# Dot products of the seventh attention tile behind the sixth tile, fixed attention steps in the first two blocks, and first halo columns on VectorE

## The chip, the cores and the metric

The kernel runs on one core of one Trainium2 chip. The metric is the device time of one execution in microseconds (us). Five engines work in parallel, each through its own queue in order: TensorE (PE: matrix products into PSUM), VectorE (DVE), ScalarE (ACT), GpSimd (POOL) and SyncE (SP, which issues the DMA transfers here). They wait for one another through semaphores.

## What is computed

Three stages follow each other: a linear attention with a decaying state, a gated feed-forward mixer with a convolution over three time steps, and a normalised feed-forward mixer with a residual.

```python
# B, H, S, D = 4, 8, 768, 48; d_model = 384, d_ff = 1024
for t in range(S):                                  # attention
    cur = einsum('bhd,bhe->bhde', u * k[t], v[t])
    y[:, :, t] = einsum('bhd,bhde->bhe', r[t], state + cur)
    state = w * state + einsum('bhd,bhe->bhde', k[t], v[t])
h = maximum(x @ w_in, 0)                            # mixer 1, x is y
conv = sum over taps 0..2 of conv_w[tap] * h shifted by tap - 1 (zeros at the ends of a sequence)
x = (h * sigmoid(conv)) @ w_out
xn = (x - mean) / sqrt(var + 1e-6) * g_ln           # mixer 2
out = x + maximum(xn @ w_ch1, 0) @ w_ch2
```

## The kernel before, in words

**Tiles and blocks.** Time is cut into 24 attention tiles of 128 steps (index n from 0, six to a sequence; the sixth tile is n = 5, the seventh n = 6). Mixer 1 works in eight blocks of 384 steps, that is of three tiles (index j), mixer 2 in six blocks of 512. Every product of the mixers is made three times, of high and low parts (`xh` and `xl`, `wih` and `wil`, `gh` and `gl`), for precision.

**Mixer 1.** For each of eight slices f, nine matmuls fill `psm` (here called an up product); ScalarE takes the positive part (`h`) and the middle tap (`c`), VectorE adds the two other taps (L474, `c<-h,tables,c`), ScalarE takes the sigmoid, VectorE multiplies by `h` (L455), ScalarE and VectorE split the result into `gh` (L460) and `gl` (L461), and nine matmuls add it into `acc` (a down product), which runs two to three slices behind the up products. An up product reads the block's three tiles and one column more on either side, the halo. `halos` (L279) copies that column between the blocks' tiles or sets it to zero, all of it on GpSimd (lines 284 to 290).

**Attention.** The function `attention` is a generator; each `yield` ends a step. A tile goes through stages: its r and k are multiplied by decay tables (L347, `rk<-rk,tables`) and its diagonal is made; then the dot products (`dps`, eight matmuls) with their mask; then the product `yps` that gives `xh` and `xl`. `state_update` (matmuls `pst`) carries the state to the next tile. Tiles below LIGHT = 6 take a form that leaves more to GpSimd and ScalarE; from tile 6 on ScalarE writes eight diagonal blocks (L358) and VectorE the masked copies (L363). For a tile n from 6 on, `decayed_k` (L249, `kks<-kt,tables`) multiplies its k by tables, twice as wide as before.

**The order around the change.** The first tiles run alone; then `after1`, called sixteen times in a mixer-1 block, advances `attention` by one step whenever a running sum `pace` passes 5: six steps in block 0 (calls 3, 6, 8, 11, 14 and 16) and seven in block 1. The weights are decoded alongside from packed words (`wdec`, `wil`, `wol`; VectorE, with a part on GpSimd and ScalarE). Matmuls stand on TensorE in program order; instructions called through `vo`, `ao`, `so` and `go` keep program order too, while a scheduler that estimates times places the others (`v_`, `a_`, `g_`, `nc.sync`) among them.

Of the kernel before, what the change touches and what calls it, by code (L numbers as in the profile page):

```python
# [35 lines left out]
LAG = 3  # L36
EARLY = 4
LIGHT = 6
GC = 16
GE = 4  # L40
SMALL = 3 * NP + KT
# [7 lines left out]
def body(ctx, tc, r, k, v, w, u, w_in, conv_w, w_out, g_ln, w_ch1, w_ch2, rkT, krv, small, out):  # L49
    nc = tc.nc  # L50
# [14 lines left out]
    g_ = nc.gpsimd  # L65
# [12 lines left out]
    vo = InOrder(nc.vector)  # L78
# [129 lines left out]
    def wdo(count=1, last=None):  # L208

        for _ in range(count):  # L210
            while w_done[0] < (len(wjobs) if last is None else last + 1):
                wload(w_done[0] + 2)
                if next(wjobs[w_done[0]][1], "end") != "end":
                    break
                w_done[0] += 1

    def need(job):
        while w_done[0] <= job:
            wdo()
# [4 lines left out]
    def load_tile(n):  # L224
# [6 lines left out]
        nc.sync.dma_start(out=rk.rearrange("x a p c -> x (a p c)"), in_=rkT[n])  # L231
        c0 = DM if n < LIGHT else 0
        nc.sync.dma_start(out=rv[:, c0:], in_=krv[n, :, DM + c0:])
# [10 lines left out]
    def decayed_k(n):  # L244

        if n < LIGHT:
            v_.tensor_tensor(out=kks[:, n % 2, 0, :, 0:D], in0=loaded[n][1], in1=tku[:, 0], op=ALU.mult)
            return
        v_.tensor_tensor(out=kks[:, n % 2, :, :, 0:D], in0=loaded[n][1].unsqueeze(1).to_broadcast([128, 2, H, D]), in1=tku,  # L249
                         op=ALU.mult)  # L250
# [28 lines left out]

    def halos(n, xh, xl):  # L280
        i, j = n % TPB, n // TT
        for t, e in ((xh, 0), (xl, 1)):
            if i == 0:
                g_.memset(t[:, :, 0:1].bitcast(F32), 0.0)
            if i == TPB - 1:
                g_.memset(t[:, :, T + 1:T + 2].bitcast(F32), 0.0)
            if n % TT == 0 and i > 0:
                g_.tensor_copy(out=xT[j - 1][e][:, :, T + 1:T + 2], in_=t[:, :, 1:2].bitcast(F32))  # L288
                g_.tensor_copy(out=t[:, :, 0:1], in_=xT[j - 1][e][:, :, T:T + 1].bitcast(F32))
# [51 lines left out]
    def attn_tile(n):  # L341
# [4 lines left out]
        rT, kT = rk[:, 0], rk[:, 1]  # L346
        (v_ if n < LIGHT else vo).tensor_tensor(out=rk, in0=rk, in1=trk, op=ALU.mult)  # L347
        if n < LIGHT:
            yield from light_tile(n, rk, vt, py, py_tag)
# [30 lines left out]
    def state_update(n):  # L380
        first, last = n % TPB == 0, n % TPB == TPB - 1
        vt = loaded[n][3]
        if not last:
# [10 lines left out]
            if n % TPB < TPB - 2:  # L394
                state[0] = ap.tile([PR, NP, D], F32, tag="sw", name="sw")
                (g_ if n < LIGHT else v_).tensor_tensor(out=state[0], in0=sn, in1=w128.to_broadcast([PR, NP, D]),
                                                        op=ALU.mult)
# [4 lines left out]
    def attention():  # L402

        tiles = {}

        def go_on(n):
            if 0 <= n < NT:
                next(tiles.setdefault(n, attn_tile(n)), None)

        go_on(0)  # L410
        decayed_k(1)
        go_on(0)
        go_on(1)
        for n in range(NT):
            state_update(n)
            go_on(n - 1)
            if n + 1 != EARLY:
                go_on(n + 1)
            yield
            go_on(n)  # L420
            go_on(n + 2 if n + 1 < EARLY else n + 1)
            yield

# [142 lines left out]
    def general_path(gctx):  # L566
# [5 lines left out]
        def gen_tile(shape, tag, bufs=2):  # L572
            return gp.tile(shape, F32, tag=tag, name="g" + tag, bufs=bufs)
# [13 lines left out]
        def load(src, c, dst):  # L587
            flat = src.rearrange("b h t d -> (b h) t d")
            for q in range(GE):
                nc.sync.dma_start(out=dst[q * B * H:(q + 1) * B * H], in_=flat[:, bass.ds(c, GC), :])  # L590

        with tc.For_i(0, S, GC) as c:
            rg = gen_tile([P, GC, D], "r")
            kg = gen_tile([P, GC, D], "k")
            uk = gen_tile([P, GC, D], "uk")
            vg = gen_tile([P, GC, EQ], "v")
            yg = gen_tile([P, GC, EQ], "y")
# [126 lines left out]


    feed = attention()

    def step():
        next(feed, None)
# [23 lines left out]
        wdo(2, wo_job[0])  # L753
    for _ in conv_weights(cst):
        pass
    ahead, pace = [iter(())], [0]
    for j in range(NB):
        slot = [0]
        while finished[0] < min((j + 1) * TT - (j % 2), NT - 1):
            step()  # L760

        def before1(f):
            if f < NF1:
                need(wi_job[f // 4])
            if f >= LAG - 1:
                need(wo_job[f - LAG + 1])

        def after1(f):
            slot[0] += 1
            pace[0] += (1.9, 2)[j] if j < 2 else 1.875  # L770
            if j == 1:
                pace[0] += 0.4
            if pace[0] >= 5:
                pace[0] -= 5
                step()
            if j == 0:
                wdo(2, wo_job[NF1 - 1])
            else:
                wdo(slot[0] % (8, 4, 3)[max(j - 5, 0)] == 2, c2_job[3])
            if j == NB - 1:  # L780
                if slot[0] == 1:
                    ahead[0] = prefetch(0)
                elif slot[0] >= 7:
                    next(ahead[0], None)

        mixer1(xT[j], spill(j), before1, after1)
# [91 lines left out]
```

## Time and profile before

| | us |
|---|---|
| median of 3 runs | 656.79 (654.98 to 658.22) |
| the profiled execution, its own time | 656.28 |
| its span | 654.6 |
| TensorE busy in the span | 625.6 (96%) |
| VectorE busy | 415.7 (64%) |
| ScalarE busy | 303.2 (46%) |
| GpSimd busy | 107.4 (16%) |
| first up product of block 0 begins | 45.96 |
| first up product of block 1 begins | 92.69 |
| first up product of block 2 begins | 136.66 |

Times in the trace count from the start of the span. The shares are means over stages with different limits: VectorE is busy for little of the second half and for nearly all of the stretch that the change touches. A matmul's width says little of the clock; the same matmul at half the granted clock stands out by its duration.

### The profile page before, as it was taken

Reading aid. Unit: us, or ns where it says so; the run is one execution under the profiler, and the core shown is the slowest. Engines: PE = TensorE matmul, PEld = TensorE weight load, DVE = VectorE, ACT = ScalarE, POOL = GpSimd, SP = SyncE. Lnnn points to the kernel's source line nnn. Section 1 sums busy time; section 2 is a strip of 40 time slices with the busy share of each in tenths; the row PEclk is TensorE's granted clock in tenths of the full one; section 3 lists DMA queues with packets and bytes.
Section 4 is the critical chain, followed back from the end, with each engine's and each line's share of the span. In section 5 each row is a group of like instructions: output and inputs, shape, how many; then the busy total and the mean of one; then the engine's idle time right before and its main releaser. Section 6 shows DMA issues by size and latency. Waiting matters only on the chain.

```text
span 654.6 us, 11766 instructions
## 1 busy us (share of the span) xinstructions
PE 625.6 (96%) x4782; PEld 573.1 (88%) x4782; DVE 415.7 (64%) x772; ACT 303.2 (46%) x662; POOL 107.4 (16%) x124
## 2 busy tenths in 40 slices
PE   5969689999999999999999999999999999999996
PEld 4859678999998999999999999999999999999995
DVE  6778999999998999978987934323322422422111
ACT  3456886778787778766855511211211221111110
POOL 5475530110020011003136501000100100100000
PEclk9998798999999999999999999999999999999998
DMA  8567615435253433103235202003001101100001
GB/s 261 148 198 244 181 54 160 132 105 174 82 164 127 134 97 98 46 28 106 87 96 168 63 0 97 2 0 97 1 0 51 47 1 49 49 1 14 35 1 53
DMA packets 25295, 56.50 MB, mean 86 GB/s; under 512 B 2961, under 2 KB 15378, under 8 KB 25234
## 3 DMA queue, kind: packets, MB, share of 16 engines
q1 hardware_dynamic: 25234, 55.68, 27.4%
q8 instruction: 39, 0.64, 0.4%
q14 instruction: 22, 0.18, 0.1%
HBM read 46.24 MB, written 9.44 MB: 85 GB/s over the span
## 4 chain that ended last, share of the span: by engine, by line
PE 82%; DVE 12%; DMA 2%; issue 1%; ACT 1%; POOL 1%; SPq 0%; ACTq 0%; DVEq 0%
PE acc L75 36%; PE psm L75 35%; PE yps L75 5%; PE dps L75 3%; DVE wdec L75 3%; DVE c L474 2%; PE pst L75 2%; PE pxt L75 1%; DVE c L455 1%; DMA rv<-in_krv_dram 1%; DMA x1b<-x_dram 1%; DVE gl L461 1%; PE pa L75 1%; DVE rk L347 1%; DVE aT L363 1%
## 5 line engine op out<-in xcount | busy, mean ns | idle before, releaser
L488 DVE SCALAR_TENSOR_TENSOR rl<-psm,rh 128x512 fp32r<-128x512 f32 x72 | 49.6, 689 | 133.7 <-ACT rh L487 130.1
L487 ACT ACTIVATE rh<-psm 128x512 fp32r<-128x512 f32 x72 | 43.1, 599 | 194.0 <-PE psm L75 190.4
L75 PE MATMUL acc<-c2h,rh 128*128 128x384 f32 x288 | 97.1, 337 | 0.0
L75 PE MATMUL acc<-c2l,rh 128*128 128x384 f32 x288 | 97.0, 337 | 0.0
L75 PE MATMUL acc<-c2h,rl 128*128 128x384 f32 x288 | 97.0, 337 | 0.0
L75 PE MATMUL psm<-xnh,c1h 128*128 128x512 f32 x216 | 86.5, 401 | 0.0
L474 DVE SCALAR_TENSOR_TENSOR c<-h,tables,c 128x384 f32<-128x384 f32 x128 | 79.9, 630 | 9.0 <-ACT c L472 8.6
L75 PE MATMUL psm<-xnh,c1l 128*128 128x512 f32 x216 | 84.9, 393 | 0.0
L75 PE MATMUL psm<-xnl,c1h 128*128 128x512 f32 x216 | 84.8, 393 | 0.0
L75 PE MATMUL psm<-xh,wih 128*128 128x386 f32 x192 | 69.2, 361 | 0.8 <-ACT aT L313 0.6
L75 PE MATMUL psm<-xl,wih 128*128 128x386 f32 x192 | 66.7, 347 | 2.4 <-POOL xl L288 2.4
L75 PE MATMUL acc<-woh,gl 128*128 128x384 f32 x192 | 65.5, 341 | 3.3 <-DVE gl L461 3.2
L75 PE MATMUL acc<-woh,gh 128*128 128x384 f32 x192 | 66.6, 347 | 0.3 <-ACT gh L460 0.3
L75 PE MATMUL psm<-xh,wil 128*128 128x386 f32 x192 | 66.6, 347 | 0.0
L75 POOL TENSOR_SCALAR wdec<-wdec 128x768 f32<-128x768 f32 (+2 forms) x19 | 55.5, 2924 | 64.2 <-ACT wdec L75 34.0
L75 PE MATMUL acc<-wol,gh 128*128 128x384 f32 x192 | 64.8, 338 | 0.0
L75 PEld LDWEIGHTS acc<-c2l,rh 128*128 128x128 f32 x288 | 54.1, 188 | 3.0
L75 PEld LDWEIGHTS acc<-c2h,rh 128*128 128x128 f32 x288 | 54.1, 188 | 2.8
L75 PEld LDWEIGHTS acc<-c2h,rl 128*128 128x128 f32 x288 | 54.0, 188 | 0.0
L511 POOL TENSOR_TENSOR rs<-rs,nhalf 128x1 f32<-128x1 f32 x24 | 16.0, 673 | 209.9 <-DVE rs L510 203.5
L75 PEld LDWEIGHTS psm<-xnh,c1l 128*128 128x128 f32 x216 | 40.6, 188 | 9.2
L75 PEld LDWEIGHTS psm<-xnl,c1h 128*128 128x128 f32 x216 | 40.7, 188 | 6.2
(116 smaller groups left out, 1132.7 us busy)
## 6 DMA issues: line engine op xcount, KB each, us to landing
rk<-in_rkT_dram SPq DMA_DIRECT2D x24, 448.0 KB, 4.5
st<-in_moe_w_ch_dram SPq DMA_DIRECT2D x12, 768.0 KB, 5.7
rv<-in_krv_dram SPq DMA_DIRECT2D x18, 448.0 KB, 4.9
kt<-in_krv_dram SPq DMA_DIRECT2D x24, 192.0 KB, 2.7
x_dram<-x SPq DMA_DIRECT2D x24, 192.0 KB, 2.0
x1b<-x_dram SPq DMA_DIRECT2D x24, 192.0 KB, 3.6
out_dram<-x1b SPq DMA_DIRECT2D x24, 192.0 KB, 2.0
st<-in_moe_w_in_dram SPq DMA_DIRECT2D x6, 512.0 KB, 7.0
```

What stands on the lines that cost most here:

```text
L75: return lambda *args, **kw: tc.keep_in_program_order(op(*args, **kw))
L347: (v_ if n < LIGHT else vo).tensor_tensor(out=rk, in0=rk, in1=trk, op=ALU.mult)
L363: v_.copy_predicated(out=aT[:, q], mask=later.bitcast(I32).unsqueeze(1).to_broadcast([128, NP, C]), data=dps[q])
L455: v_.tensor_tensor(out=st["c"], in0=st["h"][:, 1:T + 1], in1=st["c"], op=ALU.mult)
L461: v_.tensor_tensor(out=st["gl"], in0=st["c"], in1=st["gh"].bitcast(F32), op=ALU.subtract)
L474: v_.scalar_tensor_tensor(out=c, in0=h[:, o:o + T], scalar=cw[:, tap, f:f + 1], in1=c, op0=ALU.mult, op1=ALU.add)
L487: a_.activation(out=gh[:, 0:cols], in_=ps[:, 0:cols], func=AF.Relu)
L488: v_.scalar_tensor_tensor(out=gl_[:, 0:cols], in0=ps[:, 0:cols], scalar=0.0, in1=gh[:, 0:cols].bitcast(F32), op0=ALU.max, op1=ALU.subtract)
L511: g_.tensor_tensor(out=rs[:, 1:2], in0=rs[:, 0:1], in1=nhalf, op=ALU.pow)
```

## The change

Three edits. `halos` uses VectorE, in program order, for tiles below EARLY = 4 (the zero column of tile 0 and the copies between blocks 0 and 1) and GpSimd for the rest. In `attention` tile 6 is begun after tile 5 is finished: its product of r and k with the tables is no longer made in the step of tile 4's last stage, and its dot products no longer in the step of tile 5's `yps`, but in two steps behind that. And blocks 0 and 1 take their steps at fixed calls of `after1`, five and ten of them in place of six and seven; `pace` begins at 3.2 and counts from block 2 on, with the same increment there.

```diff
+STEPS = (3, 6, 8, 11, 14), (1, 3, 4, 6, 7, 9, 10, 12, 14, 16)
...
     def halos(n, xh, xl):
         i, j = n % TPB, n // TT
+        g_ = vo if n < EARLY else nc.gpsimd
...
             state_update(n)
             go_on(n - 1)
-            if n + 1 != EARLY:
+            if n + 1 not in (EARLY, LIGHT):
                 go_on(n + 1)
             yield
             go_on(n)
+            if n + 1 == LIGHT:
+                yield
+                go_on(n)
+                go_on(n + 1)
+                yield
             go_on(n + 2 if n + 1 < EARLY else n + 1)
             yield
...
-    ahead, pace = [iter(())], [0]
+    ahead, pace = [iter(())], [3.2]
...
-            pace[0] += (1.9, 2)[j] if j < 2 else 1.875
-            if j == 1:
-                pace[0] += 0.4
-            if pace[0] >= 5:
-                pace[0] -= 5
+            pace[0] += 1.875 if j > 1 else 0
+            if pace[0] >= 5 or j < 2 and slot[0] in STEPS[j]:
+                pace[0] -= 5 if j > 1 else 0
                 step()
```

By the start of block 2 both kernels have issued the same stages of the same tiles. The rows below show the instructions as they stand on an engine; the number behind a name is the buffer's, and line numbers are higher by one or more in the changed kernel.

VectorE before the first up product, kernel before: `kks_91<-kt_723` is `decayed_k` of tile 7, `sn_618` the state behind tile 4, `kks_91<-kt_579` `decayed_k` of tile 6, `wdec_631` the decoding of the convolution's weights.

```order
L75 TENSOR_TENSOR wol_96<-wdec_468,woh_95 128x768
L249 TENSOR_TENSOR kks_91<-kt_723,tables_84 128x16x48
L393 TENSOR_TENSOR sn_618<-pst_609,sw_536 112x192
L249 TENSOR_TENSOR kks_91<-kt_579,tables_84 128x16x48
L75 TENSOR_SCALAR wdec_631<-wdec_631 128x24
```

The same place in the changed kernel; `xh_309` and `xl_310` are the parts of block 0, `xh_575` and `xl_576` those of block 1.

```order
L76 TENSOR_TENSOR wol_96<-wdec_468,woh_95 128x768
L250 TENSOR_TENSOR kks_91<-kt_723,tables_84 128x16x48
L395 TENSOR_TENSOR sn_618<-pst_609,sw_536 112x192
L76 CAST xh_309<-xh_575 128x3
L76 CAST xh_575<-xh_309 128x3
L250 TENSOR_TENSOR kks_91<-kt_579,tables_84 128x16x48
L76 CAST xl_310<-xl_576 128x3
L76 CAST xl_576<-xl_310 128x3
L76 TENSOR_SCALAR wdec_631<-wdec_631 128x24
```

The four halo copies have moved from GpSimd into this row: those of `xh` stand behind the first wide `kks`, those of `xl` behind the second.

VectorE around tile 6's product of r and k (`rk_578`), kernel before; `wil_94<-wdec_755` is the last part of `wil` that the fifth up product needs, and `dps_896` belongs to tile 6.

```order
L474 SCALAR_TENSOR_TENSOR c_777<-h_776,tables_84,c_777 128x384 x2
L75 TENSOR_TENSOR wil_94<-wdec_755,wih_93 128x512
L474 SCALAR_TENSOR_TENSOR c_830<-h_829,tables_84,c_830 128x384
L75 TENSOR_SCALAR wdec_787<-wdec_787 128x768
L75 TENSOR_TENSOR rk_578<-rk_578,tables_84 112x1024
L455 TENSOR_TENSOR c_777<-h_776,c_777 128x384
L474 SCALAR_TENSOR_TENSOR c_830<-h_829,tables_84,c_830 128x384
L75 SCALAR_TENSOR_TENSOR wdec_787<-st_760,wdec_787 128x768
L363 COPY_PREDICATED aT_802<-tables_84,dps_896 128x512
```

In the changed kernel `wil_94<-wdec_755` stands ahead of both taps of the third slice, and 27 instructions further on stands `rk_578`:

```order
L481 SCALAR_TENSOR_TENSOR c_991<-h_990,tables_84,c_991 128x384
L76 TENSOR_TENSOR wol_96<-wdec_799,woh_95 128x768
L76 TENSOR_SCALAR wdec_883<-wdec_883 128x768
L462 TENSOR_TENSOR c_942<-h_941,c_942 128x384
L481 SCALAR_TENSOR_TENSOR c_991<-h_990,tables_84,c_991 128x384
L468 TENSOR_TENSOR gl_948<-c_904,gh_947 128x384
L76 TENSOR_TENSOR rk_578<-rk_578,tables_84 112x1024
L76 SCALAR_TENSOR_TENSOR wdec_883<-st_826,wdec_883 128x768
```

So `rk_578` has moved from the third slice's taps to behind `gl` of the fifth. On TensorE the dot products of tile 6 have moved from between the fourth and fifth up products to between the seventh and eighth.

## Rows read from the trace of the kernel before

**Rows 1.** Waits of TensorE: total us, times, longest.

```profile
PE dps L75 <- DVE rk L75: 5.4, 1, 5.4
PE acc L75 <- DVE gl L461: 3.2, 3, 1.9
```

**Rows 2.** Stretches: length, each engine's busy us (instructions), PE clock, DMA.

```profile
53.00:74.00 21.00, 15.01 (x194) 13.59 (x194) 19.54 (x31) 17.90 (x43) 12.94 (x7) 0.91 0.65 201
74.00:94.00 20.00, 20.00 (x168) 18.59 (x165) 20.00 (x33) 14.38 (x33) 8.23 (x5) 0.91 0.33 100
104.00:141.00 37.00, 37.00 (x412) 34.37 (x411) 35.77 (x64) 29.71 (x75) 5.39 (x7) 1.00 0.47 145
```

**Rows 3.** Waits of VectorE from 53.1 to 140.7: total us, times, longest.

```profile
DVE c L474 <- ACT c L472: 3.8, 3, 2.2
```

**Rows 4.** Timeline, TensorE, first up product: start, us, instruction, idle before.

```profile
45.96 0.44 PE L75 MATMUL psm<-xh,wih 128*128 128x386 f32 x1 [0.27 <-POOL xh L288]
48.79 0.69 PE L75 MATMUL psm<-xl,wih 128*128 128x386 f32 x1 [2.39 <-POOL xl L288]
```

**Rows 5.** Timeline, VectorE, same place, and the first convolution tap.

```profile
47.11 1.58 DVE L249 TENSOR_TENSOR kks<-kt,tables 128x768 f32<-128x768 f32 x1 [1.87 <-DMA kt<-in_krv_dram]
48.61 0.34 DVE L393 TENSOR_TENSOR sn<-pst,sw 112x192 f32<-112x192 f32 x1
48.88 0.94 DVE L249 TENSOR_TENSOR kks<-kt,tables 128x768 f32<-128x768 f32 x1
...
53.05 1.63 DVE L474 SCALAR_TENSOR_TENSOR c<-h,tables,c 128x384 f32<-128x384 f32 x2 [2.23 <-ACT c L472]
```

**Rows 6.** Timeline, GpSimd, same place.

```profile
47.05 0.82 POOL L318 TENSOR_TENSOR va<-rv,a 128x384 f32<-128x384 f32 x1
...
47.86 0.88 POOL L288 CAST xl<-xl 128x3 fp32r<-128x3 f32 x1
```

**Rows 7.** Timeline, TensorE, dot products of tile 6 and what follows.

```profile
72.64 2.08 PE L75 MATMUL dps<-rk 48*128 48x128 f32 x16 [5.41 <-DVE rk L75]
74.64 0.69 PE L75 MATMUL psm<-xh,wih 128*128 128x386 f32 x1
...
77.65 0.34 PE L75 MATMUL acc<-woh,gh 128*128 128x384 f32 x1
...
79.22 0.34 PE L75 MATMUL psm<-xh,wih 128*128 128x386 f32 x1
```

**Rows 8.** Timeline, VectorE, ahead of those dot products.

```profile
69.76 0.68 DVE L75 TENSOR_TENSOR wil<-wdec,wih 128x512 fp32r<-128x512 f32 x1
...
71.36 1.22 DVE L75 TENSOR_TENSOR rk<-rk,tables 112x1024 f32<-112x1024 f32 x1
```

**Rows 9.** Timeline, ScalarE, same place.

```profile
68.80 0.64 ACT L75 ACTIVATE wih<-wdec 128x512 fp32r<-128x512 f32 x1
...
71.28 2.44 ACT L358 ACTIVATE aT<-tables,a 128x128 f32<-128x128 f32 x8
```

**Rows 10.** VectorE's groups from 74 to 94: count, busy us, mean ns of one.

```profile
L75 DVE SCALAR_TENSOR_TENSOR wdec<-st,wdec 128x768 int32<-128x768 int32 x5 | 4.7, 943 | 0.0
L363 DVE COPY_PREDICATED aT<-tables,dps 128x512 f32<-128x512 int32 x4 | 2.8, 720 | 0.0
L75 DVE TENSOR_TENSOR wol<-wdec,woh 128x768 fp32r<-128x768 f32 x2 | 1.9, 944 | 0.0
L461 DVE TENSOR_TENSOR gl<-c,gh 128x384 fp32r<-128x384 f32 x3 | 1.6, 542 | 0.0
L75 DVE TENSOR_TENSOR rk<-rk,tables 112x1024 f32<-112x1024 f32 x1 | 1.2, 1209 | 0.0
L75 DVE TENSOR_SCALAR wdec<-wdec 128x768 int32<-128x768 int32 x2 | 1.1, 548 | 0.0
```

**Rows 11.** The page's costliest groups: VectorE's convolution taps, whole span.

```profile
L474 DVE SCALAR_TENSOR_TENSOR c<-h,tables,c 128x384 f32<-128x384 f32 x128 | 79.9, 630 | 9.0 <-ACT c L472 8.6
```

**Rows 12.** Timeline, VectorE: first tap of block 2's first slice.

```profile
140.72 0.61 DVE L474 SCALAR_TENSOR_TENSOR c<-h,tables,c 128x384 f32<-128x384 f32 x1
```

## The prediction

> **What bounds the kernel now.** I read the waits of TensorE first, since it is busy for nearly all of the span: what it can give back is what it stands still, and almost all of that lies ahead of 104 us. The longest wait behind the start is 5.4 us for VectorE's product of r and k, ahead of the dot products of tile 6; `gl` costs 3.2 us in three places [rows 1]. The timeline of the first up product shows the other wait that the change addresses: 0.27 us for the halo of `xh` and 2.39 us for that of `xl`, both from GpSimd [rows 4]. Each is followed by slow matmuls. Behind the 5.41 us wait nine matmuls take 3.01 us (74.64 to 77.65), while the nine after them take 1.57 us (77.65 to 79.22) [rows 7]: 1.4 us more, at the lower of the clock's two levels for most of it. So the stall at tile 6 costs 6.8 us with that, and the dot products behind it, slow too, some tenths more.
>
> Then I asked what the engine that is waited for was doing. The stretches show it: VectorE is busy 19.5 us of 21 from 53 to 74, 20.0 of 20 from 74 to 94 and 35.8 of 37 from 104 to 141 [rows 2]. In the 87.7 us from the first convolution tap at 53.05 [rows 5] to the first tap of block 2 at 140.72 [rows 12] its waits for ScalarE's `c` are 3.8 us in three, and the longest, 2.2 us, is the one that ends at 53.05 [rows 3, 5]. So it stands still for some 1.6 us in there, with a few tenths elsewhere. **VectorE bounds this stretch; TensorE's waits are where that shows.** An edit that only reorders work can give back VectorE's idle time and no more, except for what TensorE's lead over it allows.
>
> **The halos.** GpSimd loses four copies and two zero columns, VectorE gains them. In the changed order the copies of `xh` stand behind the wide `kks` of tile 7 and `sn`, those of `xl` behind the wide `kks` of tile 6 as well. The first `kks` waits 1.87 us for its DMA and starts at 47.11; `sn` starts at 48.61, the second `kks` at 48.88 [rows 5]. Nothing ahead of them changes, so the transfer lands at the same time. The copy of `xh` can start at 48.9, that of `xl` a `kks` later (0.94 us long), at 49.9 to 50.0. A three-column copy on VectorE has no row here; it costs between nothing and the 0.34 us of `sn`, and since it holds three columns against 192, I take 0.1. TensorE's first matmul goes from 45.96 to 49.0 and the second, the one that counts, from 48.79 to 50.1. **That is 1.3 us later**; between 0.9 and 2.0 with the bounds. The first tap, which waits for that up product through ScalarE, goes from 53.05 to about 54.35. The clock's cost stays, since the engine again stands idle just before.
>
> One rule speaks to the size. The first `kks` takes 1.58 us and the second 0.94 [rows 5], and GpSimd's `va` runs from 47.05 to 47.87 beside the first [rows 6]. The Trainium skill, page "SBUF — State Buffer", section "SBUF: two separate sides", says that a VectorE instruction with two SBUF inputs and a GpSimd instruction share a port pair as a lock, so that the later one waits for the whole of the earlier. The two rows agree with it. With GpSimd relieved of its copies `va` would end some 0.3 us earlier, and by that rule, as an estimate, the halos would cost 1.0 us in place of 1.3 and the whole 658.1.
>
> **Tile 6.** Ahead of the fifth up product TensorE now meets no dot products; it needs the last part of `wil` instead. That stood at 69.76 and the product of r and k behind it at 71.36 [rows 8]. In the changed order `wil` stands ahead of both taps, but it still needs ScalarE's `wih`, which starts at 68.80 [rows 9]; with 1.3 us of delay VectorE waits there 1 to 1.4 us and `wil` ends near 70.8. The fifth up product then ends near 71, some 6 us earlier than before. This is the gain, and the question is what is late next.
>
> From `wil` to the decoded `wol` that the next but one down product needs stand eleven instructions: four taps of 0.63, two decode steps of 0.94, one of 0.55, two gates and one `gl` of 0.54, `wol` 0.94 [rows 10, 11], together 7.5 us, less 0.07 for each that starts before the former ends (48.61 and 0.34 against 48.88 [rows 5]): 6.8. ScalarE adds some 1.0, since its eight diagonal blocks of tile 7 (2.44 us [rows 9]) now stand ahead of the sigmoid of the third slice. So `wol` is ready near 78.6. TensorE then has a down, an up and a down product to the new place of the dot products, 1.6 us each: 83.4. But tile 6's product of r and k is 27 instructions behind `wil`: ten taps (6.3), four long decode steps (3.8), three short (1.6), four gates and three `gl` (3.8), two `wol` (1.9) and itself (1.2) make 18.6, less 1.9 for the overlap, 16.7; with ScalarE's 1.0 it ends near 88.5. **TensorE waits there for 5 us again**, with a slow clock after it. The wait has moved with the instruction.
>
> **The steps.** Three steps (one and a half tiles) move from block 0 to block 1. Nothing is added to any engine but the copies: to the first tap of block 2 VectorE has the same instructions to do, one `gl` more (0.5). What counts is therefore VectorE's clock at that tap: 87.7 less the 1.6 it waited is 86.1; with 0.5 more, the start at 54.35 and 1.4 and 1.0 of new waits it comes at 143.3, 2.6 us later than 140.72. TensorE is busy for all of 104 to 141 [rows 2], so VectorE's results lie ready for it there, and part of the 2.6 is taken out of that lead. How much no row says; it lies between nothing and all, and I take 1.0. From block 2 on `pace` starts lower and shifts steps by one product; TensorE is full there and its work the same, so I cost that at nothing (0.5 either way).
>
> **The sum.** Plus 1.3 for the halos, 0.5 for the `gl`, 2.4 for the new waits, less 1.6 of old ones and 1.0 of lead: +1.6 us. On the profiled execution's 656.28 that is 657.9; the median of the runs is 0.5 above that execution, and on it 658.4, which I predict. Its own range is 655 to 661: 1.1 us of halo bounds, 1.0 of lead and a new wait or two either way.
>
> **The rivals.**
> *The stall goes.* If TensorE, having passed the fifth up product 6 us earlier, finds its next operands in time, the 6.8 us are won and only the halos are paid: 656.8 - 6.8 + 1.3 = 651.3; had the halos been won too (2.66 us of waiting), 647.3. Against it stands VectorE's 20.0 of 20 us [rows 2]; for it that the moved steps take 1.2 us of `rk` and two masks of 0.72 [rows 10] out of that stretch. It needs TensorE's lead in block 1 to be several us. Chance 0.18.
> *Block 1 gets too full.* Ten steps stand where seven stood, beside a VectorE with 1.2 us free in 37 [rows 2]. The moved stages are one `rk`, two masks, one `kks` and about five of half a us: some 4.7 us. If block 0 gives none of that back, because VectorE waits for ScalarE there, block 1 lasts 4.7 - 1.2 = 3.5 us longer on top of the 1.3: 661.6. It decides from the point at which VectorE loses more than 2 us to waits between 54 and 97. Chance 0.27.
> *The halos' delay is hidden*, the rest as forecast: 657.1, inside the forecast's range. If instead both edits simply cancel, 656.8. Both are counted in the forecast's 0.55.
>
> **How the numbers follow.** The forecast holds 0.55, the first rival 0.18, the second 0.27. The range that should hold eight times in ten reaches down to the first rival's 651.3 and up to the second's 661.6 with an us for its size: 651.0 to 662.8. A measurement of this kernel tells about 0.5%, 3.3 us, from no change: 653.5 to 660.1. Faster takes the first rival and 0.02 of the forecast: 0.20. Slower takes four fifths of the second and 0.05 of the forecast: 0.27. Within: 0.53.
>
> **What would show it.** In the changed profile the second matmul of the first up product starts at 49.7 to 50.8, with its wait put down to VectorE; if it starts before 48.8, the halo step is wrong. The fifth up product ends near 71 and the dot products of tile 6 start at 86 to 90 after several us of waiting; if they start by 84, VectorE was not the bound and the first rival holds. The tap of block 2's first slice comes at 141.5 to 144. If waits pile up ahead of dot products and products `yps` between 98 and 137, it is the second rival. A gain at unchanged VectorE idle time would overturn the whole argument.

## The result: slower by one per cent, four times the loss forecast

The changed kernel takes 663.72 us in the median of six runs (662.59 to 665.85), the kernel before 657.08 in six beside them: the ratio is 1.0102, with a 95% interval of 1.0076 to 1.0128. A second measurement gave 662.41 against 656.79, 1.0095 (1.0076 to 1.0113). Forecast was +1.6 us; by the ratios it came to +6.7 and +6.2. The profiled execution of the changed kernel is its longest run (665.85, span 664.0), so differences between the two traces add up to more than the medians do: 9.4 us. Of these some 3 lie at 217 us and in part come and go between runs; in the second measurement the profiled run has a span of 660.7.

| start of | before | changed | changed, again |
|---|---|---|---|
| second matmul of the first up product | 48.79 | 50.03 | 49.98 |
| second up product of block 0 | 51.53 | 52.77 | 52.72 |
| first up product of block 1 | 92.69 | 97.44 | 97.45 |
| first up product of block 2 | 136.66 | 140.85 | 140.87 |
| first up product of block 4 | 208.94 | 214.67 | 214.13 |
| span | 654.6 | 664.0 | 660.7 |

So, between these traces, 1.2 us are lost at the halos and 3.5 more in the rest of block 0; block 1 gives 0.6 back; some 1.5 to 2 us are lost at 149 us in block 2, and the rest in stalls further on.

### The profile page after: what moved, and what is told of

It reads as the page before. It is cut to its first block, busy times and chain, and to the rows that moved or that the text cites. A ratio compares the mean times of both kernels' runs of the same rounds, so it can differ in the third digit from the quotient of the medians.

```text
span 664.0 us, 11785 instructions
## 1 busy us (share of the span) xinstructions
PE 627.8 (95%) x4782; PEld 575.3 (87%) x4782; DVE 417.0 (63%) x778; ACT 302.7 (46%) x662; POOL 103.8 (16%) x118
## 4 chain that ended last, share of the span: by engine, by line
PE 84%; DVE 7%; DMA 4%; ACT 2%; issue 2%; SPq 1%; DVEq 0%; ACTq 0%
PE acc L76 37%; PE psm L76 37%; PE yps L76 4%; PE dps L76 3%; DMA rk<-in_rkT_dram 2%; DVE wdec L76 2%; PE pst L76 1%; PE pxt L76 1%; DVE c L481 1%; DMA rv<-in_krv_dram 1%; DMA x1b<-x_dram 1%; DVE gl L468 1%; DVE rk L349 0%; DVE c L462 0%; DVE wil L76 0%
## 5 line engine op out<-in xcount | busy, mean ns | idle before, releaser
L478 ACT ACTIVATE h<-psm 128x386 f32<-128x386 f32 x64 | 31.3, 490 | 39.2 <-PE psm L76 39.0
```

The costliest lines, as they stand in the source:

```text
L478: a_.activation(out=h, in_=ps[:, 0:T + 2], func=AF.Relu)
```

## The profile after

TensorE's waits, whole span, changed kernel (total us, times, longest), the answer to [rows 1]:

```profile
PE dps L76 <- issue: 7.2, 2, 5.4
...
PE acc L76 <- DVE gl L468: 3.3, 2, 2.2
PE psm L76 <- DVE xh L76: 3.0, 1, 3.0
PE acc L76 <- ACT gh L467: 2.0, 1, 2.0
```

The 5.4 us wait ahead of dot products is still there, as long as in [rows 1]; the view names no releaser for it, but VectorE's `rk` ends at 90.32 and they start at 90.43, as the timelines below show. Halos now cost 3.0 us ahead of the first matmul instead of 2.4 ahead of the second. Timeline of TensorE, changed kernel, answering [rows 4] and [rows 7], with the start of block 2, the wait behind it, and the stall at 217 us:

```profile
49.11 0.66 PE L76 MATMUL psm<-xh,wih 128*128 128x386 f32 x1 [2.96 <-DVE xh L76]
50.03 0.69 PE L76 MATMUL psm<-xl,wih 128*128 128x386 f32 x1 [0.26 <-DVE xl L76]
...
84.70 0.33 PE L76 MATMUL acc<-woh,gl 128*128 128x384 f32 x1
90.43 2.08 PE L76 MATMUL dps<-rk 48*128 48x128 f32 x16 [5.39 <-issue]
92.43 0.69 PE L76 MATMUL psm<-xh,wih 128*128 128x386 f32 x1
...
97.44 0.34 PE L76 MATMUL psm<-xh,wih 128*128 128x386 f32 x1
...
140.85 0.45 PE L76 MATMUL psm<-xh,wih 128*128 128x386 f32 x1
...
150.96 1.16 PE L76 MATMUL dps<-rk 48*128 48x128 f32 x16 [1.81 <-issue]
...
218.95 0.53 PE L76 MATMUL acc<-woh,gl 128*128 128x384 f32 x1 [2.17 <-DVE gl L468]
```

Eighteen microseconds later than in [rows 7], the same picture: a stand of 5.4 us, dot products at the lower clock (2.08 us against the 1.16 of those at 150.96; the granted clock is 0.50 from 90.43 to 95.49), an up product that takes 3.06 us to its down product at 95.49. VectorE's timeline, answering [rows 5], [rows 8] and [rows 12]:

```profile
47.29 0.96 DVE L250 TENSOR_TENSOR kks<-kt,tables 128x768 f32<-128x768 f32 x1 [1.59 <-DMA kt<-in_krv_dram]
48.18 0.34 DVE L395 TENSOR_TENSOR sn<-pst,sw 112x192 f32<-112x192 f32 x1
48.44 0.59 DVE L76 CAST xh<-xh 128x3 fp32r<-128x3 f32 x2
48.95 0.95 DVE L250 TENSOR_TENSOR kks<-kt,tables 128x768 f32<-128x768 f32 x1
49.82 0.25 DVE L76 CAST xl<-xl 128x3 fp32r<-128x3 f32 x2
...
54.18 1.65 DVE L481 SCALAR_TENSOR_TENSOR c<-h,tables,c 128x384 f32<-128x384 f32 x2 [3.28 <-ACT c L479]
...
70.16 0.69 DVE L76 TENSOR_TENSOR wil<-wdec,wih 128x512 fp32r<-128x512 f32 x1 [1.58 <-ACT wih L76]
...
89.11 1.21 DVE L76 TENSOR_TENSOR rk<-rk,tables 112x1024 f32<-112x1024 f32 x1
...
96.91 1.27 DVE L481 SCALAR_TENSOR_TENSOR c<-h,tables,c 128x384 f32<-128x384 f32 x2 [0.87 <-ACT c L479]
...
148.45 0.62 DVE L481 SCALAR_TENSOR_TENSOR c<-h,tables,c 128x384 f32<-128x384 f32 x1 [0.47 <-ACT c L479]
```

The four copies stand behind the two `kks`, as the order showed. `rk` ends at 90.32. Seven microseconds later VectorE waits for its next tap, because the eighth up product stood behind the dot products and came late. Block 2's first tap is at 148.45 instead of 140.72.

The stretches of [rows 2] in the changed kernel (length, busy us of TensorE, its weight loads, VectorE, ScalarE, GpSimd with their instructions, then TensorE's clock and the DMA's share):

```profile
53.00:74.00 21.00, 19.79 (x211) 17.93 (x210) 17.99 (x30) 17.87 (x41) 12.37 (x7) 0.94 0.60 192
74.00:94.00 20.00, 11.34 (x52) 10.00 (x52) 19.01 (x30) 12.05 (x24) 7.44 (x3) 0.80 0.34 106
104.00:141.00 37.00, 37.00 (x494) 33.28 (x487) 35.34 (x64) 28.34 (x75) 1.94 (x6) 1.00 0.41 127
```

VectorE, 39.54 us of 41 in the first two stretches before, is now at 37.0. Cut at the places that belong together, first tap to block 1 and block 1 to block 2, the kernel before:

```profile
53.05:92.69 39.64, 33.65 (x351) 30.82 (x350) 38.23 (x61) 30.92 (x69) 20.37 (x10) 0.91 0.51 157
92.69:136.66 43.97, 41.78 (x485) 37.58 (x482) 42.90 (x77) 32.95 (x85) 3.41 (x8) 0.96 0.44 133
```

and the changed kernel:

```profile
54.18:97.44 43.26, 33.39 (x272) 30.18 (x271) 39.57 (x61) 30.24 (x64) 19.95 (x11) 0.87 0.45 145
97.44:140.85 43.41, 43.41 (x561) 39.05 (x560) 40.61 (x72) 31.83 (x82) 1.94 (x6) 1.00 0.36 112
```

These four lines hold most of the answer. Three attention steps have left block 0, yet it is 3.6 us longer: VectorE is idle for 3.7 us of it instead of 1.4 and busy for 1.3 more. And block 1, which took those steps in, has a TensorE without any idle time: 43.41 us of 43.41. The 2.2 us in which TensorE stood still there before are gone, block 1 is 0.6 us shorter, and it can't give back more of block 0's loss. VectorE's waits from its first tap to that of block 2, changed kernel (the 3.3 us are those that end at the first tap):

```profile
DVE c L481 <- ACT c L479: 4.2, 2, 3.3
DVE c L462 <- ACT c L461: 1.7, 3, 0.7
DVE wil L76 <- ACT wih L76: 1.6, 1, 1.6
DVE kks L250 <- DMA kt<-in_krv_dram: 0.9, 1, 0.9
DVE gl L468 <- ACT gh L467: 0.9, 2, 0.5
DVE kks L250 <- PE pst L76: 0.5, 1, 0.5
```

VectorE's whole account between these taps, the kernel before and then the changed one (columns as above):

```profile
53.05:140.72 87.67, 79.49 (x854) 72.47 (x854) 85.02 (x143) 67.83 (x160) 26.46 (x18) 0.94 0.46 141
54.18:148.45 94.27, 84.40 (x907) 76.58 (x909) 86.81 (x144) 68.61 (x162) 24.11 (x18) 0.94 0.41 130
```

So before, 87.67 us held 2.65 of idle time; here 94.27 us hold 7.46. In the second measurement 93.77 us hold 6.54.

## The experiments

Ratios are to the kernel before, run beside each on the same chip, with the 95% interval. A difference from the changed kernel is one of ratios, at 657 us.

| label | ratio (interval) | us from before | block 1 from | block 2 from | second up product of block 0 to block 2 |
|---|---|---|---|---|---|
| before | 1 | 0 | 92.69 | 136.66 | 85.13 |
| changed | 1.0102 (1.0076 to 1.0128) | +6.7 | 97.44 | 140.85 | 88.08 |
| after_again | 1.0095 (1.0076 to 1.0113) | +6.2 | 97.45 | 140.87 | 88.15 |
| e1_halos_vector | 1.0025 (1.0009 to 1.0042) | +1.6 | 96.46 | 138.41 | 85.83 |
| e3_after_halos_gpsimd | 1.0079 (1.0053 to 1.0105) | +5.2 | 94.85 | 138.20 | 87.21 |
| e8_before_steps_moved | 1.0031 (1.0014 to 1.0047) | +2.0 | 91.99 | 137.71 | 85.72 |
| e6_after_rk_early | 1.0027 (1.0008 to 1.0047) | +1.8 | 90.27 | 136.94 | 85.35 |
| e9_after_dots_later | 1.0060 (1.0037 to 1.0083) | +3.9 | 90.35 | 138.09 | 85.59 |
| e10_after_tap_out0 | 1.0044 (1.0026 to 1.0063) | +2.9 | 95.22 | 138.59 | 85.70 |
| e11_after_tap_out1 | 1.0073 (1.0058 to 1.0088) | +4.8 | 98.34 | 141.74 | 89.22 |
| e4_after_phase38 | 1.0086 (1.0059 to 1.0113) | +5.7 | 96.93 | 140.33 | 88.08 |
| e5_before_phase32 | 1.0022 (1.0001 to 1.0043) | +1.4 | 92.86 | 136.93 | 85.17 |
| c2_halos_scalar_first | 0.9974 (0.9957 to 0.9992) | -1.7 | 93.73 | 135.74 | 86.49 |
| c3_after_scalar_first | 1.0013 (0.9994 to 1.0033) | +0.9 | 88.75 | 133.35 | 84.61 |
| c4_rk_early_scalar | 1.0031 (1.0010 to 1.0051) | +2.0 | 92.03 | 136.95 | 86.92 |
| c5_rk_early_scalar38 | 0.9999 (0.9975 to 1.0022) | 0 | 93.08 | 137.63 | 88.60 |
| c6_dots_later_scalar | 1.0003 (0.9982 to 1.0025) | +0.2 | 89.40 | 136.23 | 86.31 |
| c7_scalar_dots_one_later | 1.0015 (1.0000 to 1.0031) | +1.0 | 97.89 | 137.60 | 89.47 |

The columns of times are from one profiled execution each. The start-up differs between executions by up to 1.2 us (with the same order up to there, the second matmul starts at 50.03 in the changed kernel and at 48.86 in e6), which the last column leaves out. A start of block 2 is no forecast of the time by itself: c3 starts it 3.3 us before the kernel before, but VectorE's first tap of block 2 comes at 140.86 there, as late as before (140.72), and the time is +0.9.

### One edit at a time: halos, and the rest without them

e1 is the kernel before with this line, e3 the changed kernel without it:

```diff
         i, j = n % TPB, n // TT
+        g_ = vo if n < EARLY else nc.gpsimd
```

> The kernel before with one edit: the first halos (tiles 0 to 3) are copied by VectorE. Theory of three costs: the halos alone delay the second matmul of the first up product from 48.79 to about 50.0 us (the changed kernel has 50.03), nothing later gives that back, and the time is 657.1 + 1.2 = 658.3 us. Rival (the delay is absorbed, since VectorE waits 2 to 3 us for its first tap anyway and the whole loss belongs to the moved dot products): second matmul at 50.0 too, but the time stays at 657.1 us, and the start of the first up product of block 2 (136.66 us before) does not move.

> The changed kernel with the halos back on GpSimd, so the moved product and dot products and the ten steps alone. Theory of three costs: second matmul at 48.8 us again, the wait of about 5.4 us before the seventh tile's dot products remains (they start near 89.2 us), and the time is 663.7 - 1.2 = 662.5 us. Rival (halos absorbed): 663.7 us. A second rival (halos are all of the loss): 657 us.

TensorE's timeline in e1, the second matmul:

```profile
49.84 0.69 PE L75 MATMUL psm<-xl,wih 128*128 128x386 f32 x1 [0.27 <-DVE xl L75]
```

e1 costs 1.6 us (0.6 to 2.8), as the theory had it, and the second matmul comes where it was expected. That the whole 1.6 lies at this matmul is not shown: the section on the prediction comes back to it. Without the halos 5.2 us remain. Both single costs add up to 6.8, the whole. The dot products in e3:

```profile
87.98 2.08 PE L76 MATMUL dps<-rk 48*128 48x128 f32 x16 [5.14 <-DVE rk L76]
```

The wait is the same without the halos, and here the view names VectorE's product.

### The three steps moved, without tile 6's product

```diff
+STEPS = (3, 6, 8), (1, 3, 4, 6, 7, 9, 10, 12, 14, 16)
...
-            pace[0] += (1.9, 2)[j] if j < 2 else 1.875
-            if j == 1:
-                pace[0] += 0.4
-            if pace[0] >= 5:
-                pace[0] -= 5
+            pace[0] += 1.875 if j > 1 else 0
+            if pace[0] >= 5 or j < 2 and slot[0] in STEPS[j]:
+                pace[0] -= 5 if j > 1 else 0
```

with `pace` from 3.8, on the kernel before.

> The kernel before with the changed kernel's places for the steps (three in block 0 and ten in block 1, phase 3.8 behind them), while the seventh tile's product and dot products stay where they were and the halos stay on GpSimd: only the move of three steps from block 0 to block 1. Theory (starving): the 5.4 us wait ahead of the dot products stays near 73 us, the moved steps cost nothing by themselves, the first product of block 2 starts at 136 to 138 us and the time is 657 us, 1 either way. Rival (block 1 is too full with ten steps): TensorE or VectorE lengthens block 1 by about 3.5 us, the first product of block 2 starts near 140 us, and the time is 660.5 us.

It lies between: +2.0 us. Block 0 gives back 1.2 us for the three steps (40.00 from its second up product to block 1, before 41.16), block 1 takes 1.75 more (45.72, before 43.97). A fuller block 1 is thus a price, but 3.5 us was too much, and it does not explain 5.2.

### Tile 6's product back in its place, its dot products not

```diff
-            if n + 1 not in (EARLY, LIGHT):
+            if n + 1 != EARLY:
                 go_on(n + 1)
...
             if n + 1 == LIGHT:
                 yield
                 go_on(n)
-                go_on(n + 1)
                 yield
```

> The changed kernel with the seventh tile's product of r and k back in its old place (behind the fifth tile's part of the same step), while its dot products stay in their new place behind the sixth tile. Theory (starving: in the changed kernel TensorE stands 5.4 us ahead of these dot products, no up product is made meanwhile, and VectorE runs dry behind it): the dot products start near 85.5 us without a long wait, VectorE's waits between 54 and 148 us fall from 7.5 to about 4, the first product of block 2 starts near 138 us instead of 140.9, and the time is 663.7 - 3 = about 660.7 us. Rival (VectorE's amount of work sets the pace, as the prediction had it): TensorE gets as much waiting for gl and wol instead, the first product of block 2 starts at 140 to 141 us, and the time stays at 663.7 us.

The dot products in TensorE's timeline:

```profile
85.91 1.16 PE L76 MATMUL dps<-rk 48*128 48x128 f32 x16
```

No wait, the higher clock, and 4.5 to 4.9 us off the time, more than expected. VectorE's idle time between the taps falls from 7.5 to 5.1 us. **The late place of this one product of 1.2 us is what costs most.** The rest of that stage did not move with it: in both kernels ScalarE begins the diagonal blocks of two tiles at 64 to 65 and at 71 to 72 us. With the product early, halos, ten steps and late dot products together are only 1.8 us slower than before.

### The product late, the dot products later still

```diff
-STEPS = (3, 6, 8, 11, 14), (1, 3, 4, 6, 7, 9, 10, 12, 14, 16)
+STEPS = (3, 6, 8, 11), (1, 2, 3, 4, 6, 7, 9, 10, 12, 14, 16)
```

> The changed kernel with the seventh tile's dot products moved on by one more up and down product (they follow the eighth up product instead of preceding it); its product of r and k stays in its new, late place on VectorE, and block 1 gets eleven steps, the first of which holds these dot products. Theory (starving: what the changed kernel loses there is that TensorE stands ahead of the dot products while the eighth up product, which needs nothing of them, stands behind): the eighth up product starts near 85 us instead of 92.4, the wait ahead of the dot products falls from 5.4 to under 2 us, the first product of block 2 starts at 137.5 to 139 us, and the time is 663.7 - 3 = about 661 us. Rival (the late place of the product in VectorE's row, or the fuller block 1, is the cost): TensorE waits as long for gl and wol, and the time is 663 to 664 us.

TensorE's timeline, eighth up product and dot products:

```profile
85.28 0.34 PE L76 MATMUL psm<-xh,wih 128*128 128x386 f32 x1
...
92.03 1.16 PE L76 MATMUL dps<-rk 48*128 48x128 f32 x16
```

The product of r and k is as late as in the changed kernel; what differs is that TensorE makes the eighth up product meanwhile. It starts 7.2 us earlier, VectorE's idle time is 4.5 us instead of 7.5, and 2.3 to 2.8 us of the loss are gone, as expected. So that part of the harm is in standing with work behind: while TensorE waits at the head of its queue, nothing is made that VectorE could go on with. The wait is not all gone: in e9 TensorE stands 2.7 us at 101.40, ahead of the next tile's dot products. Some 2 us lie between e9 and e6; block 1, with eleven steps, lasts 47.7 us in e9 and 46.7 in e6, which is half of it, and the rest isn't traced.

### Less work for VectorE, in block 0 and in block 1

```diff
+        made[0] += 1
-        for tap, o in ((0, 0), (2, 2)):
+        for tap, o in ((0, 0), (2, 2))[(made[0] - 1) // NF1 == 0:]:
```

with `== 1` for block 1; `made` counts up products. The first tap is left out of eight slices, so the convolution there is another one.

> The changed kernel once more, to be compared with the others of this call on one chip: ratio 1.0102 to the kernel before, as first measured, within 1.0076 to 1.0128.

> The changed kernel with the first tap of the convolution left out in the eight slices of block 0 (its result is then another): VectorE has 8 x 0.63 = 5.0 us less to do there, TensorE nothing less. Theory (VectorE sets the length of block 0, by its work and by the waits for ScalarE that lie in its chain): most of it comes off, the first product of block 2 starts at 136 to 138 us instead of 140.9, and the time is 3 to 5 us below the changed kernel. Rival (TensorE's stand ahead of the seventh tile's dot products sets it): VectorE's idle time rises by as much as its work falls, and the time is at most 1 us lower.

> The changed kernel with the first tap left out in the eight slices of block 1 instead. Theory (VectorE bounds block 1 too, as the prediction had it): the first product of block 2 starts at 137 to 139 us, and the time is 4 to 5 us below the changed kernel. Rival (with ten steps in it TensorE bounds block 1, since it has no idle time from 94 to 149 us): the first product of block 2 stays at 140 to 141 us, only the 1.8 us wait at 149 us goes, and the time is 2 us lower.

Of the 5.0 us taken from VectorE in block 0, 2.2 show at the start of block 1 and 3.4 in the time: VectorE does set that block, not for every microsecond. The stand ahead of the dot products shrinks with its work, from 5.2 us in the second measurement to 4.0, so this run does not part the two. The same 5.0 us taken from block 1 change its length by nothing: 43.40 us (98.34 to 141.74) against 43.42 (97.45 to 140.87). Stretch of e11, columns as above, and the only wait that TensorE has there from 94 to 210 us:

```profile
94.00:141.00 47.00, 47.00 (x567) 42.75 (x567) 42.16 (x73) 34.06 (x87) 2.00 (x8) 0.96 0.40 118
```

```profile
PE dps L76 <- ACT c L481: 0.2, 1, 0.2
```

Here the rival is right: **in the changed kernel TensorE bounds block 1**. The ten steps alone don't do that: with ten steps too, TensorE stands still for 2.6 us of block 1 in e8 and 3.0 in e6, and VectorE for only 0.9 and 1.1. The wait at 149 us is gone in e11, so there VectorE was late out of block 1; e11's time is 1.4 us lower by the ratios, whose intervals overlap.

### The phase of the steps from block 2 on

e4 is the changed kernel with `pace` from 3.8; e5 the kernel before with 0.6 taken off once at the start of block 2.

> The changed kernel with the pace of the steps from block 2 on started at 3.8, where the kernel before stands at that point, instead of 3.2. Theory of three costs: the waits of TensorE at 149 us (1.8 us) and at 217 us (2.2 us, and a slow clock behind it) hang on the phase of the steps and go, up to the first product of block 2 nothing changes (140.9 us), and the time is 663.7 less 2 to 5 us, near 660 us. Rival (VectorE comes late out of block 1 and the later waits are its arrears, whatever the phase): 663.7 us, with a wait of 1 to 2 us near 149 us.

> The kernel before with the phase of the changed one from block 2 on: 0.6 is taken off the pace once, at the first call in block 2. Theory of three costs: nothing changes up to 137 us, a wait of TensorE of 2 us or more for a gl product appears in 205 to 215 us behind a VectorE product that waits for the load of rv, and the time is 657.1 + 2 to 4 = about 660 us. Rival (the phase costs nothing by itself, as the prediction had it): 657.1 us and no new wait.

In e4 the wait at 149 us stays (1.67 us), so it isn't the phase; the one at 217 is gone, and the time is 0.6 to 1.0 us lower, less than the intervals can tell. e5 measures +1.4 us (0.1 to 2.8), and its trace has a new wait for `gl`, at 212.21; in the kernel before TensorE is busy for 10.83 us of the 11 from 205 to 216. The wait is shorter than expected, and VectorE meets no late load ahead of it:

```profile
212.21 0.45 PE L75 MATMUL acc<-woh,gl 128*128 128x384 f32 x1 [1.45 <-DVE gl L461]
```

c5, below, is c4 with 3.8 in place of 3.2 and comes out 2.1 us lower. So three pairs point the same way, 0.6 to 2.1 us against the phase of the change, each near the limit of what its intervals can tell. Waits of 1.2 and 1.1 us for `gl` also stand at 214 us in e1 and at 210 in e8, whose phase is that of before, so the phase is not all. In the changed kernel VectorE's product `av` is held up by a load, with `gl` behind it:

```profile
217.87 0.56 DVE L354 TENSOR_TENSOR av<-kks,rv 128x384 f32<-128x384 f32 x1 [1.70 <-DMA rv<-in_krv_dram]
218.34 0.55 DVE L468 TENSOR_TENSOR gl<-c,gh 128x384 fp32r<-128x384 f32 x1
```

The same kernel's second trace has 0.50 us there instead of 1.70, and a wait of TensorE of 0.95. Why the load is late only in some executions and orders stays open; it is worth 1 to 3 us of an execution.

### Halos on ScalarE

ScalarE writes `xh` and `xl` for these tiles itself, so its own copies need no other engine. The second edit brings them ahead of ScalarE's copies of the state, which wait for VectorE.

```diff
+    def halo_copy(out, in_):
+        a_.activation(out=out, in_=in_, func=AF.Copy)
...
-                g_.tensor_copy(out=xT[j - 1][e][:, :, T + 1:T + 2], in_=t[:, :, 1:2].bitcast(F32))
-                g_.tensor_copy(out=t[:, :, 0:1], in_=xT[j - 1][e][:, :, T:T + 1].bitcast(F32))
+                copy = halo_copy if n < EARLY else g_.tensor_copy
+                copy(out=xT[j - 1][e][:, :, T + 1:T + 2], in_=t[:, :, 1:2].bitcast(F32))
+                copy(out=t[:, :, 0:1], in_=xT[j - 1][e][:, :, T:T + 1].bitcast(F32))
...
         for n in range(NT):
+            if n == EARLY:
+                go_on(n - 1)
             state_update(n)
```

c2 is this on the kernel before, c3 on the changed kernel in place of its halos.

> The kernel before with two edits: the halo copies of tiles 0 to 3 are made by ScalarE, which writes the halos' sources itself, and the last part of the fourth tile is issued ahead of the fifth tile's state update, so that ScalarE makes these copies ahead of its copies of the state. Theory (the first up product waits only for the engine that copies): the second matmul of the first up product starts at 46.6 to 47.2 us instead of 48.79, the first tap at 51.2 instead of 53.05, all that follows comes 1.8 us earlier, and the time is 657 - 1.8 = 655.2 us. Rival (the 1.8 us are lost again, since the tap coefficients come at 50.8 us and VectorE's or ScalarE's later waits take the rest): second matmul as early, time 657 us.

> The changed kernel with the first halos made by ScalarE and the fourth tile's last part ahead of the fifth tile's state update, instead of the halos on VectorE. Theory (the halos' cost is the start of the first up product and adds to the rest): second matmul at 46.6 to 47.2 us instead of 50.03, and the time is 663.7 - 3 = 660.7 us. Rival (the start is not what counts behind the 5.4 us wait ahead of the seventh tile's dot products): 663 to 664 us.

ScalarE's timeline in c2:

```profile
46.01 0.51 ACT L340 ACTIVATE xl<-yps 128x384 fp32r<-128x384 f32 x1
46.55 0.21 ACT L281 ACTIVATE xl<-xl 128x3 fp32r<-128x3 f32 x1
```

and TensorE's:

```profile
46.81 0.69 PE L75 MATMUL psm<-xl,wih 128*128 128x386 f32 x1
...
72.29 2.08 PE L75 MATMUL dps<-rk 48*128 48x128 f32 x16 [8.91 <-DVE rk L75]
74.30 0.69 PE L75 MATMUL psm<-xh,wih 128*128 128x386 f32 x1
```

c2 beats both kernels: 0.9974 (0.9957 to 0.9992), 1.7 us. The second matmul comes 2.0 us earlier, as expected; 0.9 us of that are left at block 2. Its second number matters as much: TensorE waits 8.9 us ahead of tile 6's dot products, 3.5 more than before, and the kernel is faster. In that place the wait costs little: VectorE, which has weights to decode beside it, is idle for 3.6 us between the second up product and block 1, before 2.9 and in the changed kernel 5.1. c2 holds two edits; GpSimd's or VectorE's copies with the last part of tile 3 brought forward in the same way were not tried.

c3 gained 5.4 to 5.8 us on the changed kernel where 3 were expected: with the earlier start and another order on VectorE the wait ahead of the dot products falls to 3.5 us. So the two costs are not independent after all.

### Putting them together

c4 is e6 with the ScalarE halos, c5 the same from 3.8, c6 is e9 with the ScalarE halos. c7 is c2 with the steps at fixed calls, (3, 6, 9, 11, 14, 16) and (2, 4, 7, 9, 11, 13, 15), which puts tile 6's dot products behind the fifth up product.

> The changed kernel with the seventh tile's product of r and k in its old place, and with the first halos made by ScalarE ahead of its copies of the state. If the two effects measured singly add (+0.27% with the product back, halos 0.5% better on ScalarE than on VectorE): 657 + 1.8 - 3.0 = 655.8 us, below the kernel before. Rival (a lead at the start is lost again by block 2, as the run of the changed kernel with ScalarE's halos lost 7 of its 10 us of lead): 657 us.

> The same with the pace from block 2 on started at 3.8. If the phase works here as it did on the changed kernel (a wait for gl near 217 us that goes, about 1 us in the median): 1 us below the kernel with phase 3.2, so 654.8 us. Rival (that wait depended on how late VectorE came out of block 1, and not on the phase): the same time as with phase 3.2.

> The changed kernel with the seventh tile's dot products behind the eighth up product and the first halos on ScalarE. Theory of starving, and effects that add: 661 - 3 = 658 us. Rival (as in the changed kernel with ScalarE's halos, which measured +0.13%, the start alone already removes most of the wait): no further gain from the later dot products, 657.5 us.

> The kernel before with the first halos on ScalarE (the kernel of 0.9974) and the step that holds the seventh tile's dot products one call later, behind the fifth up product. Theory (TensorE's wait of 8.9 us ahead of them only shows VectorE's bound): the wait falls to 5 us or less, VectorE's idle time in block 0 by at most 1 us, and the time is 0 to 1 us below the kernel of 0.9974. Rival (the wait is what the kernel loses): 3 to 5 us below it, near 652 us.

None beats c2. c4 missed by 3 us: it starts 1.6 us before e6 and reaches block 2 at the same time. c5 and c6 equal the kernel before; c5 missed its forecast by 2 us. In c7 the wait ahead of the dot products is 4.9 us instead of 8.9, and it is 2.7 us slower than c2:

```profile
PE psm L76 <- ACT wih L76: 5.9, 2, 4.0
PE dps L76 <- issue: 4.9, 1, 4.9
```

TensorE now waits 5.9 us for the decoded `wih` in the same stretch. A wait of TensorE moved about in block 0 is no measure of a gain.

## Why the prediction was wrong, and where it was right

**Halos: the mechanism right, the size in part luck.** Second matmul 50.1 forecast, 50.03 measured; first tap 54.35 and 54.18; 1.3 us of cost, 1.24 between the traces and 1.6 in the time of e1. The lock rule of the Trainium skill, page "SBUF — State Buffer", section "SBUF: two separate sides", has whichever starts first, a GpSimd instruction or a VectorE one with two SBUF inputs, keep the shared ports until it ends; by it the prediction's estimate was 1.0. The traces agree with the rule, with the roles exchanged in the changed kernel: GpSimd's product no longer begins first, so `kks` takes 0.96 us, not the 1.58 of [rows 5], and GpSimd's `va` takes 1.53, not the 0.82 of [rows 6]:

```profile
47.41 1.53 POOL L320 TENSOR_TENSOR va<-rv,a 128x384 f32<-128x384 f32 x1
```

The 0.6 us that `kks` won went to the copies (0.59 us for the two of `xh`, where 0.2 was forecast) and to a later transfer (47.29 against 47.11).

What the prediction could not see is that the kernel before has a second outcome here. In [rows 5] and [rows 6] `va` begins 0.06 us ahead of `kks`. e5 keeps the order of the kernel before on TensorE, VectorE, ScalarE and GpSimd up to 149 us, and there `kks` begins first:

```profile
46.38 1.03 DVE L249 TENSOR_TENSOR kks<-kt,tables 128x768 f32<-128x768 f32 x1 [1.61 <-DMA kt<-in_krv_dram]
46.58 1.52 POOL L318 TENSOR_TENSOR va<-rv,a 128x384 f32<-128x384 f32 x1
49.02 0.69 PE L75 MATMUL psm<-xl,wih 128*128 128x386 f32 x1 [3.09 <-POOL xl L288]
```

The second matmul then starts 2.64 us behind `kks`, as in e3 (2.64) and e8 (2.67), where the halos are GpSimd's too; in the trace of the kernel before it is 1.68, in the changed kernel 2.74. So VectorE's halos cost 1.06 us here against the one outcome and 0.1 against the other. How often each comes, and where the rest of e1's 1.6 us lies, no run says.

**The wait moves with the instruction: right.** `wil` ends at 70.85 (70.8 forecast), `wol` at 78.61 (78.6), a wait of 5.4 us stands ahead of the dot products (5 forecast). They start at 90.43, not 88.5, just outside the 86 to 90 given: `rk` ends 19.5 us behind `wil`, not 17.7. The wait has its forecast length since TensorE arrives late too, at 85.04, not 83.4; that much is luck.

**The sum of waits: the step that failed.** VectorE's clock to block 2's first tap was the right thing to add up. In the eleven kernels e1, e3, e6, e8, e9 and c2 to c7 VectorE is busy for 85.4 to 87.6 us between these taps (85.0 before) and idle for 3.6 to 6.1; TensorE stands still for 8.4 to 12.6, most of all in c2, the fastest. But the term for the idle time was too small. Forecast was a tap 2.6 us later: 1.3 for the start, 0.5 more busy, and 0.8 more idle, 2.4 us of new idle time against 1.6 of old. Measured are 1.1, 1.8 and 4.8 (idle 7.46 against 2.65), and the tap came at 148.45, not 143.3; in the second measurement they are 1.1, 2.2 and 3.9. What the prediction left out is the way back: it costed the wait for VectorE as TensorE's alone, "where that shows". In [rows 7] that holds, since VectorE has decoding to do (c2). At 85 to 90 us of the changed kernel it doesn't: TensorE stands with the eighth up product behind it, and VectorE runs short behind that. From 85 to 100 us it is idle for 2.1 us (1.6 in the second measurement), in the kernel before for none, in e6 and e9, which remove the stand in two ways, for 0.4 and 0.1; these two bring back 2.3 to 4.9 us of the time. That is some 2 of the 4.8. Of the rest, 1.3 lie ahead of 85 us, where the wait for `wih` was forecast as 1.0 to 1.4 and took 1.58, and 1.4 behind 100; no run takes these apart.

**The lead: the size met, by luck.** One us was taken off because VectorE's results lie ready for TensorE. The tap came 7.7 us later (7.2 in the second measurement) and the time 6.7 (6.2), so 1.0 was absorbed. But in the other kernels the tap's delay less the time's lies anywhere between -1.0 (e5) and 3.9 (c5). And TensorE itself gave nothing back to speak of: it is busy for all of 97.44 to 140.85, and e11 shows that it, not VectorE, bounds this block there.

**The pace at nothing: probably wrong.** The wait at 149 us belongs to VectorE's late arrival (e11), not to the phase (e4). The phase was put at nothing, 0.5 either way; e4, e5 and c5 give 0.6 to 1.0, 1.4 and 2.1 us for it, none of them well clear of its interval. That would be a second, smaller part of the miss.

**The rivals.** "Block 1 gets too full" came nearest, 661.6, and its point of decision was passed: VectorE's named waits between 54 and 97 are 3.3 us, more than 2. Its mechanism is half right: block 0 gave nothing back, but block 1 grew no longer, and no waits piled up in it. "The stall goes" is excluded by the 5.4 us. The measured 663.7 lies 0.9 above the upper end of the range, because that end was this rival's price, which left out what the stand costs VectorE.

## What to carry to other kernels

Before a wait is moved, ask what stands behind it on the waiting engine: if the engine that is waited for lives on that work, the wait costs both of them, and the same 5 us that were nearly free beside a backlog are dear without one. A block in which one engine is busy for every microsecond gives back nothing of what that engine lost ahead of it. And try a small copy on the engine that writes its source: ScalarE's halos, issued ahead of its copies of the state, won 2 us at the start.

## What the runs showed of the hardware that was not expected

A copy of three columns costs what its neighbours make of it: 0.19 us alone on GpSimd at 45.72 and 0.88 at 47.86 beside a VectorE `kks` [rows 6], 0.21 on ScalarE, and on VectorE two in 0.59 us ahead of a `kks` and two in 0.25 behind it. Which of `va` and `kks` begins first, by 0.06 us one way or 0.2 us the other, moves the second matmul by 1 us in one and the same order. And effects measured singly need not add: c3 gained 2 to 3 us more, c4 3 us less than their parts. The orders of VectorE and ScalarE are made anew for each kernel, which is the likely reason, not a tested one.
